# Convolution and phase mixing on one core: two more tiles for the sums, another start-up order

## Chip, cores and metric

The kernel runs on one core of a Trainium2 chip, alone on the chip. The metric is the device time of one launch in microseconds (us). The median of five runs before the change is 1427.22 us (1426.32 to 1431.56).

## What is computed

```python
# x: (8, 4224, 192); weight: (8, 7)
w = softmax(weight)                        # 7 taps for each of 8 groups of 24 channels
x = causal_convolution(x, w)               # along the 4224 tokens
theta = x @ w_theta                        # 192 x 192
zr, zi = x * cos(theta), x * sin(theta)
y = w_tok_r @ zr + w_tok_i @ zi            # 4224 x 4224, along the tokens, for each batch and channel
u = x + y
out = u + max(u @ w_ch, 0)                 # 192 x 192
```

Nearly all arithmetic is in `y`: two 4224 x 4224 matrices times 4224 x 1536 (8 batches of 192 channels).

## The kernel before

**Tiling.** The 4224 tokens are cut into 33 *chunks* of 128 tokens for the inner sum, and into 33 output tiles of 128 tokens, handled two at a time as 17 *units*. The 1536 columns are two halves of 768, and each half is worked on in two pieces of 384. A *visit* multiplies one unit with the chunks that are at hand then, at most 11 (`SLOTS`), since that many fit into on-chip memory. Visits 0 to 16 have few chunks each (`FIRST` lets in two chunks at once and then one per visit); later ones have up to 11. A unit is visited several times, and its running sum of four tiles `d` (128 x 768, fp32) goes out to `part` in DRAM between visits (`store`, L754) and comes back for the next one (`load`, L677). A scheme of the Strassen kind saves one eighth of the products: it needs sums of weights (`w`, L570) and of chunks (`t`, L437).

**Stages of a chunk.** POOL (GpSimd) issues loads of a *window* of x (three pieces of 32 tokens, each with 6 tokens of *halo* ahead of it). PE (TensorE) convolves a window by multiplying with `bands`, a banded matrix made of the taps (L321). ACT (ScalarE) and DVE (VectorE) copy the result out of the banks to `xz` (L182 to L184). It is turned by PE (L486; later chunks by DMA), multiplied with `w_theta` (L501), put through sine and cosine on ACT (L406) and multiplied with x on DVE (L416). Then come the sums `t` (L437).

**Weights.** POOL issues loads of the token weights to `st` (L534), and DVE turns them in blocks of 32 x 32 to `w` (L556).

**Products and outputs.** L715 issues the products, each 128 x 128 by 384 columns. DVE adds a finished bank to `d` (L739). After a unit's last visit the tile is output: ACT casts it to bf16 (L861) into a *container*, which holds the cast and its transpose; the transpose comes from a DMA that ACT issues (L480), or, in the last four visits, from PE; PE multiplies with `w_ch` (L501), DVE takes the maximum and adds (L880), and SP issues the store (L887). There are 5 containers (`outring`), used in turn, and 8 tiles `d`; late in the kernel two more `d` (`late`) come out of memory that the windows have left. Where a unit gets its x added, POOL loads it (`xr<-xs`, L684) and adds it to `d` (L687).

**What sets the order.** All these steps are objects with an assumed duration and a due time. A planner in the program (`Schedule`) runs through them before anything is emitted, with assumed times at which each engine starts (`START`) and at which transfers land (`LAND`), and emits the instructions of each engine in the order that this plan gives. On the chip each engine's queue is then in that fixed order, and an instruction that has to wait holds up all behind it. While the plan's clock is under 60 us (`WARM`) and PE is free in the plan, it emits small matmuls of a zero tile `noise` (128 columns, L1150) that compute nothing and keep PE active. Ahead of the first convolution stand 18 larger ones (512 columns, L981). The noise of L1150 writes into bank 0, which the products use too.

**Start-up.** DVE clears `masks` (L903) and `noise` (L905). POOL issues the first window of x (L275) and turns `masks` into a banded pattern (L912); DVE makes the taps' softmax out of `weight`, sums `masks` over three blocks (`taps`, L931), finds which of three blocks a row belongs to (`block`, a maximum over all of `masks`, L937), multiplies (`terms`, L954), adds over the 7 taps (L963), and scales by `block` to `bands` (L974 on DVE, L972 on ACT).

Of the kernel before, what the change touches and what calls it, by code (L numbers as in the profile page):

```python
# [16 lines left out]
def kernel(  # L17
# [22 lines left out]
    nc = tc.nc  # L40
# [57 lines left out]
    dpool = ctx.enter_context(tc.tile_pool(name="dpool", bufs=8))  # L98
# [113 lines left out]
    bands = constp.tile([WR, H, NQ + WQ, Q], BF16, name="bands")  # L212
# [31 lines left out]

    class Window:
# [15 lines left out]
        def halos(self):  # L261
            prev = self.prev
            for j in range(WQ):
                t0, lo = tokens(*divmod(self.m * WQ + j, NQ)) - KS + 1, j * ROWS
                if t0 < 0:
                    nc.vector.memset(xw[self.k][0 : KS - 1, :, :], 0.0)
                elif self.m < 2:
                    self.loads.append(self.load(lo, t0, KS - 1, prev))
                else:
                    self.loads.append(self.halo(j, lo, prev))  # L270
            self.uses += self.loads

        def load(self, lo, t0, n, prev):
# [6 lines left out]
            if self.m < 2:  # L280
                run()
                s = Step("none", 0.0, None)
                s.fixed = START["x"][self.m]
                return s
# [13 lines left out]
        def conv(self):  # L298
# [29 lines left out]
            for hp in range(H // 2):  # L328
                m = Step(
                    "pe", 0.17, lambda b, hp=hp: conv(b, hp), [self.loads, prevs], mm=True  # L330
# [305 lines left out]
    dtile = tiles(dpool, 8, [P, HN], F32, "d")  # L636
    dfree = [(lambda k=k: dtile[k], []) for k in range(8)]

    def container(k):
        if ("u", k) not in late:  # L640
            if k < 4:
                small_tile(0)
                tag, bufs = (("ang", 2), ("xz", 3))[k % 2]
# [8 lines left out]
    outring = Ring(5)  # L652
    last_of_part = {}

    class Visit:
# [104 lines left out]
        def products(self):  # L760
# [4 lines left out]
            for r in "xys" if self.pair else "xy":  # L765
                for g in gs:
                    k, uses[r, g], prev[r, g] = rings[r].take()
                    rows[r, g] = 2 * "xys".index(r) + k
                    if self.v == 0 and r == "x":
                        continue  # L770
# [83 lines left out]
        def output(self, q):  # L854
            k, use, prev = outring.take()
            if len(outring.uses) <= 5:
                prev = [
                    s for r in ("xz", "uT", "xw") for u in rings[r].uses[-3:] for s in u
                ]
# [36 lines left out]
    START = {"x": (7.5, 10.5), "pe": 7.5, "dve": 10.5, "act": 8.3, "pool": 8.3, "sp": 4.5, "wth": 9.0}  # L896
# [5 lines left out]
    masks = wk.tile([WR, KS, WQ, Q], BF16, name="masks", tag="ang")  # L902
    nc.vector.memset(masks, 1.0)  # L903
    noise = wk.tile([P, 512], BF16, name="noise", tag="ang")
    nc.vector.memset(noise, 0.0)  # L905
    wth_f = wk.tile([P, 4, D], F32, name="wth_f", tag="xz", bufs=3)
    nc.vector.memset(wth_f[:, 1:3, :], 0.0)
# [8 lines left out]
    windows[0].halos()  # L916
    Window()
    ident = constp.tile([P, P], BF16, name="ident")
    make_identity(nc, ident)
    windows[1].halos()  # L920
    nc.vector.memset(bands[:, :, WQ, :], 0.0)
    wmax, wsum, wrcp = (taps_f[:, 1, k * H : (k + 1) * H] for k in range(3))
    nc.vector.tensor_reduce(out=wmax, in_=wsb, axis=mybir.AxisListType.X, op=ALU.max)
    nc.vector.tensor_tensor(
        out=wsb, in0=wsb, in1=wmax[:, :].unsqueeze(2).to_broadcast([P, H, KS]),
        op=ALU.subtract,
    )
    nc.scalar.activation(out=wsb, in_=wsb, func=AT.Exp)
    taps = wk.tile([WR, KS, Q], BF16, name="taps", tag="xz", bufs=3)
    for j in range(1, WQ):  # L930
        nc.vector.tensor_tensor(  # L931
            out=taps, in0=masks[:, :, 0, :] if j == 1 else taps, in1=masks[:, :, j, :],
            op=ALU.add,
        )

    block = constp.tile([WR, WQ], F32, name="block")
    nc.vector.tensor_reduce(  # L937
        out=block, in_=masks[:, :, :, :].rearrange("p k j m -> p j k m"),
        axis=mybir.AxisListType.XY, op=ALU.max,
    )  # L940
    nc.scalar.activation(out=wmax[:, 0:1], in_=wsb[:, 0, 0:1], func=AT.Sin)
    wth_t = wk.tile([P, 4, D], BF16, name="wth", tag="wc", bufs=1)
    nc.scalar.activation(out=wth_t, in_=wth_f, func=AT.Copy)
    nc.vector.tensor_reduce(out=wsum, in_=wsb, axis=mybir.AxisListType.X, op=ALU.add)
    nc.vector.tensor_scalar_add(out=wsum, in0=wsum, scalar1=1e-9)
    nc.vector.reciprocal(out=wrcp, in_=wsum)
    wbf = wk.tile([P, H, KS], BF16, name="wbf", tag="xr")
    nc.vector.tensor_tensor(
        out=wbf, in0=wsb, in1=wrcp[:, :].unsqueeze(2).to_broadcast([P, H, KS]),
        op=ALU.mult,  # L950
    )
    terms = spool.tile([WR, KS, H, Q], BF16, name="terms", tag="st")
    for hs in (slice(0, H // 2), slice(H // 2, H)):
        nc.vector.tensor_tensor(  # L954
            out=terms[:, :, hs], in0=taps[:, :, :].unsqueeze(2).to_broadcast([WR, KS, H // 2, Q]),
            in1=wbf[0:WR, hs, :].rearrange("p h k -> p k h").unsqueeze(3).to_broadcast(
                [WR, KS, H // 2, Q]
            ), op=ALU.mult,
        )
        n = KS  # L960
        while n > 1:
            k = n // 2
            nc.vector.tensor_tensor(  # L963
                out=terms[:, 0:k, hs], in0=terms[:, 0:k, hs], in1=terms[:, n - k : n, hs],
                op=ALU.add,
            )
            n -= k
        for j in (1, 0, 2):
            o = bands[:, hs, j::NQ, :]
            i = terms[:, 0, hs].unsqueeze(2).to_broadcast([WR, H // 2, 2, Q])  # L970
            if j == 1:
                nc.scalar.activation(out=o, in_=i, func=AT.Copy, scale=block[:, j : j + 1])  # L972
            else:
                nc.vector.tensor_scalar_mul(out=o, in0=i, scalar1=block[:, j : j + 1])  # L974
    wth = lambda: wth_t
    wth_ready = Step("none", 0.0, None)
    wth_ready.fixed = START["wth"]

    for k in range(6):
        for _ in range(3):  # L980
            pe(nc.tensor.matmul(banks[k], lhsT=noise[:, 0:P], rhs=noise, start=True, stop=True))  # L981
# [62 lines left out]
    class Schedule:  # L1044


        def __init__(self, emit):
# [13 lines left out]
            self.lent = {k: 0.0 for k in range(2, 6)}  # L1061
# [54 lines left out]
        def step(self, now):  # L1116
# [30 lines left out]
            if now < WARM and self.free["pe"] <= now + 1e-9:  # L1147
                self.free["pe"] = now + 0.11
                if self.emit:
                    pe(nc.tensor.matmul(  # L1150
                        banks[0][:, 3 * P : 4 * P], lhsT=noise[:, 0:P], rhs=noise[:, 0:P],
                        start=False, stop=True, skip_group_check=True,
# [39 lines left out]
```

## Time and profile before

| | |
|---|---|
| median of 5 runs | 1427.22 us |
| the profiled execution: its time / its span | 1425.21 / 1423.5 us |
| PE busy (matmul), weight loads | 1402.1 us (98%), 892.4 us |
| DVE, ACT, POOL busy | 1039.6, 438.3, 508.0 us |
| products (L715) | 3186 + 2228 + 2162 matmuls, 326 ns each, one begun every 163 ns |
| first convolution, first product begun at | 10.76, 19.26 us |
| last noise matmuls begun at | 61.5 us |
| mean granted PE clock | 0.997 |

A line of the windows view gives a stretch of the span, its length, then for each engine the busy time and, in brackets, the number of instructions, the clock granted to PE (1.00 is full speed), the share of time in which the 16 DMA engines were busy, and GB/s. A line of the timeline gives start, duration, engine, source line, operation, tiles and count, and in square brackets how long the engine had been idle and what released it. A line of the waits gives who waited for whom, the total, the number of times and the longest, in us. The release is inferred: where a wait has several causes, only the one that came last by the profile is named.

### The profile page before, as it was taken

To read this page: it belongs to the slowest core of one execution; us is meant where nothing else is said; L and a number is where in the kernel's file an instruction comes from. 1 tells how busy PE (TensorE), PEld (TensorE's weight loads), DVE (VectorE), ACT (ScalarE), POOL (GpSimd) and SP (SyncE) were. 2 spreads that over 40 slices of the span, in tenths; PEclk is the share of its full clock that TensorE was granted. 3 is DMA by queue.
4 is the path that set the end of the run, shared out by engine and by line. 5 is a ranking of instruction groups with operands and counts; after the bars stand their busy time and mean duration, and the time that the engine had idled before them with its cause. 6 is when DMAs were issued, how large, how long until landed. Compare 5 with 4: busy or idle time off the path is not lost.

```text
span 1423.5 us, 25083 instructions
## 1 busy us (share of the span) xinstructions
PE 1402.1 (98%) x9485; PEld 892.4 (63%) x9485; DVE 1039.6 (73%) x1679; ACT 438.3 (31%) x885; POOL 508.0 (36%) x761
## 2 busy tenths in 40 slices
PE   8999999999999999999999999999999999999998
PEld 5666666666666666666666666666666665666665
DVE  7978665345777886776667688687687987887787
ACT  7875522113523323310000342233231212211232
POOL 7543311122432553223213346424545153531120
PEclk9999999999999999999999999999999999999999
DMA  9999975577999899999778999999998999999994
GB/s 132 228 203 203 168 148 105 115 129 166 221 224 237 215 229 243 225 198 216 183 166 206 226 232 241 220 256 218 219 239 168 239 227 217 268 253 197 217 247 145
DMA packets 335777, 291.43 MB, mean 205 GB/s; under 512 B 157140, under 2 KB 284500, under 8 KB 335656
## 3 DMA queue, kind: packets, MB, share of 16 engines
q0 software_dynamic: 168784, 97.61, 50.7%
q1 hardware_dynamic: 126872, 182.39, 40.9%
q10 hardware_dynamic: 40000, 9.84, 5.3%
q8 instruction: 74, 1.21, 0.3%
q14 instruction: 47, 0.39, 0.1%
HBM read 248.53 MB, written 104.99 MB: 248 GB/s over the span
## 4 chain that ended last, share of the span: by engine, by line
PE 94%; DVE 3%; DMA 2%; ACT 1%; issue 1%; POOL 1%; DVEq 0%; POOLq 0%; ACTq 0%
PE bank L715 85%; PE bank L501 6%; PE bank L321 2%; DMA ubT<-ubT 1%; PE bank L486 1%; PE bank L1150 1%; DMA out_dram<-d 0%; DVE d L880 0%; DVE d L739 0%; POOL xw L275 0%; DVE w L570 0%; DVE w L556 0%; DVE i L416 0%; ACT uT L184 0%; DVE xz L182 0%
## 5 line engine op out<-in xcount | busy, mean ns | idle before, releaser
L715 PEld LDWEIGHTS <-w 128*128 128x128 bf16 x7576 | 735.8, 98 | 458.7 <-issue 6.2
L715 PE MATMUL bank<-t,w 128*128 128x384 bf16 x3186 | 563.5, 326 | 3.3 <-DVE d L739 2.9
L739 DVE TENSOR_TENSOR d<-bank,d 128x384 f32<-128x384 f32 x528 | 285.7, 548 | 240.8 <-PE bank L715 206.6
L715 PE MATMUL bank<-i,w 128*128 128x384 bf16 x2228 | 390.6, 326 | 0.2 <-DVE bank L182 0.2
L556 DVE STREAM_TRANSPOSE w<-st 128x640 bf16<-128x640 bf16 (+4 forms) x412 | 341.3, 854 | 66.2 <-PE bank L715 53.4
L715 PE MATMUL bank<-r,w 128*128 128x384 bf16 x2162 | 388.1, 326 | 0.3
L534 POOL DMA_DIRECT2D st<-in_moe_w_tok_r_dram x240 | 137.9, 582 | 438.4 <-DVE w L556 414.3
L570 DVE TENSOR_TENSOR w<-w 128x1408 bf16<-128x1408 bf16 (+8 forms) x212 | 183.9, 867 | 2.6
L534 POOL DMA_DIRECT2D st<-in_moe_w_tok_i_dram x240 | 137.3, 579 | 130.9 <-DVE w L556 118.9
L184 ACT ACTIVATE xz<-bank 64x384 bf16<-64x384 f32 (+2 forms) x297 | 138.3, 482 | 90.6 <-issue 52.4
L275 POOL DMA_DIRECT2D xw<-in_x_dram x137 | 79.5, 587 | 177.7 <-PE bank L321 147.1
L687 POOL TENSOR_TENSOR d<-d,xr 128x768 f32<-128x768 f32 x61 | 103.6, 1700 | 100.6 <-DMA xr<-xs 54.4
L406 ACT ACTIVATE r<-bank,half_pi 128x384 bf16<-128x384 f32 x88 | 47.8, 581 | 263.4 <-PE bank L501 263.2
L184 ACT ACTIVATE bank<-bank 128x384 f32<-128x384 f32 x108 | 51.3, 477 | 219.2 <-PE bank L715 204.2
L184 ACT ACTIVATE d<-bank 128x384 f32<-128x384 f32 x122 | 59.3, 491 | 139.3 <-PE bank L715 138.5
L861 ACT ACTIVATE ubT<-d 128x768 bf16<-128x768 f32 x43 | 36.3, 844 | 146.8 <-DVE d L739 132.0
L880 DVE SCALAR_TENSOR_TENSOR d<-bank,d 128x384 f32<-128x384 f32 x106 | 54.5, 549 | 14.2 <-PE bank L501 12.4
L501 PEld LDWEIGHTS <-uT 128*128 128x128 bf16 x632 | 54.4, 98 | 12.8 <-issue 1.2
L406 ACT ACTIVATE i<-bank 128x384 bf16<-128x384 f32 x132 | 61.7, 495 | 0.0
L501 PE MATMUL bank<-wth,uT 128*128 128x192 bf16 x528 | 56.9, 246 | 0.3
L321 PE MATMUL bank<-xw,bands 114*128 114x192 bf16 x352 | 52.2, 248 | 4.3 <-DMA xw<-in_x_dram 3.2
L501 PE MATMUL bank<-wch,ubT 128*128 128x192 bf16 x424 | 45.9, 246 | 2.4 <-DMA ubT<-ubT 1.3
(75 smaller groups left out, 537.2 us busy)
## 6 DMA issues: line engine op xcount, KB each, us to landing
part<-d SPq DMA_DIRECT2D x168, 384.0 KB
d<-part SPq DMA_DIRECT2D x155, 384.0 KB
st<-in_moe_w_tok_r_dram POOLq DMA_DIRECT2D x156, 176.0 KB, 6.7
st<-in_moe_w_tok_i_dram POOLq DMA_DIRECT2D x156, 176.0 KB, 7.8
out_dram<-d SPq DMA_DIRECT2D x53, 384.0 KB
xw<-in_x_dram POOLq DMA_DIRECT2D x132, 96.0 KB, 4.7
xs<-xz SPq DMA_DIRECT2D x132, 96.0 KB
xr<-xs POOLq DMA_DIRECT2D x66, 192.0 KB, 6.4
```

What stands on the lines that cost most here:

```text
L184: act(nc.scalar.activation(out=o(), in_=i(*b), func=AT.Copy))
L275: pool(nc.gpsimd.dma_start(out=xw[self.k][lo : lo + n, :, :], in_=x[:, t0 : t0 + n, :].rearrange("b s d -> s b d"),))
L321: pe(nc.tensor.matmul(banks[b][:, hh * B * G : (hh + 1) * B * G], lhsT=bands[:, h, at : at + NQ, :].rearrange("p z m -> p (z m)"), rhs=xw[ ...
L406: act(nc.scalar.activation(out=z[:, cols], in_=banks[b][:, 0 : 2 * D], func=AT.Sin, **({"bias": half_pi[:], "scale": 1.0} if i == 0 else { ...
L501: pe(nc.tensor.matmul(banks[bk][:, b * D : (b + 1) * D], lhsT=tT[:, 3 * k + b + i, :], rhs=w[:, 2 * b + i, :], start=(i == 0), stop=(i == ...
L534: "pool", 0.58, lambda a=a, t0=t0, i=i, w=w: pool(nc.gpsimd.dma_start(out=st[i][a * Q : (a + 1) * Q, 0:nb, 0 : n * Q], in_=w[r0 : r0 + nb ...
L556: lambda c=c, ce=ce: dve(nc.vector.transpose(self.tile(name)[:, c:ce, :, :], st[i][:, at : at + NQ, c * Q : ce * Q].rearrange("p bt (c j) ...
L570: s = Step("dve", 0.15 + 0.069 * n, lambda: dve(nc.vector.tensor_tensor(out=flat(self.tile(name)), in0=flat(self.tile(p)), in1=flat(self.t ...
L687: a = Step("pool", 1.75, lambda: pool(nc.gpsimd.tensor_tensor(out=tile_(), in0=tile_(), in1=xrt[k], op=ALU.add)), [r, s])
L715: pe(nc.tensor.matmul(banks[bank][:, 0:PC], lhsT=self.w.block(a, c), rhs=chunks[c].operand(b, g), start=(start and c == self.lo), stop=(c ...
L739: dve(nc.vector.tensor_tensor(out=o, in0=y, in1=o, op=ALU.add))
L880: dve(nc.vector.scalar_tensor_tensor(out=dk, in0=banks[b][:, 0:PC], scalar=0.0, in1=dk, op0=ALU.max, op1=ALU.add,))
```

## The change

1. The tiles `d` become 10 instead of 8. The memory comes from the tag `ang` (two tiles, which held `masks`, `noise` and two of the containers). `masks` and `noise` move to tiles of other tags, and there are 4 containers instead of 5: one in the place of `bands`, two `xz`, one `uT`.
2. `block` is made on POOL, by a memset and two selects of 114 x 3, and no longer by DVE's maximum over `masks`.
3. Two of the three halos of window 1 are copied on the chip by SP out of window 0, instead of loaded by POOL from DRAM. `ident`, the identity for transposes, is made after the loads of window 1.
4. The start-up's DVE and ACT instructions are put into the fixed order (`dve(...)`, `act(...)`), and the loops that build `bands` go over the two halves of the heads in turn.
5. The first noise is 16 matmuls over all banks. Noise of the plan goes into one of the two banks that the plan uses for convolution and mixing, and only when the plan has that bank free. For window 0 and 1 and chunk 0 the plan may lend six banks instead of four.
6. `START` has other times, and the convolutions wait in the plan for `bands`.

```diff
-    dpool = ctx.enter_context(tc.tile_pool(name="dpool", bufs=8))
+    dpool = ctx.enter_context(tc.tile_pool(name="dpool", bufs=10))
...
-    bands = constp.tile([WR, H, NQ + WQ, Q], BF16, name="bands")
+    bands = wk.tile([WR, H, NQ + WQ, Q], BF16, name="bands", tag="bands", bufs=1)
...
-                elif self.m < 2:
+                elif self.m * WQ + j < NQ:
                     self.loads.append(self.load(lo, t0, KS - 1, prev))
...
-                    "pe", 0.17, lambda b, hp=hp: conv(b, hp), [self.loads, prevs], mm=True
+                    "pe", 0.17, lambda b, hp=hp: conv(b, hp), [self.loads, prevs, bands_ready],
+                    mm=True
...
-    dtile = tiles(dpool, 8, [P, HN], F32, "d")
-    dfree = [(lambda k=k: dtile[k], []) for k in range(8)]
+    dtile = tiles(dpool, 10, [P, HN], F32, "d")
+    dfree = [(lambda k=k: dtile[k], []) for k in range(10)]
...
-            if k < 4:
+            if k < 3:
                 small_tile(0)
-                tag, bufs = (("ang", 2), ("xz", 3))[k % 2]
+                tag, bufs = (('bands', 1), ('xz', 3), ('xz', 3))[k]
...
-    outring = Ring(5)
+    outring = Ring(4)
...
-                    if self.v == 0 and r == "x":
-                        continue
...
-            if len(outring.uses) <= 5:
+            if len(outring.uses) <= 4:
...
-    START = {"x": (7.5, 10.5), "pe": 7.5, "dve": 10.5, "act": 8.3, "pool": 8.3, "sp": 4.5, "wth": 9.0}
+    START = {
+        "x0": 6.3, "x1": 10.0, "bands": 9.8, "pe": 8.3, "dve": 9.6, "act": 9.8,
+        "pool": 8.4, "sp": 4.5,
+        "wth": 9.0,
+    }
...
-    masks = wk.tile([WR, KS, WQ, Q], BF16, name="masks", tag="ang")
-    nc.vector.memset(masks, 1.0)
-    noise = wk.tile([P, 512], BF16, name="noise", tag="ang")
-    nc.vector.memset(noise, 0.0)
+    noise = wk.tile([P, 512], BF16, name="noise", tag="xr")
+    dve(nc.vector.memset(noise, 0.0))
+    masks = wk.tile([WR, KS, WQ, Q], BF16, name="masks", tag="xz", bufs=3)
+    dve(nc.vector.memset(masks, 1.0))
...
     windows[0].halos()
+    block = constp.tile([WR, WQ], F32, name="block")
+    nc.gpsimd.memset(block, 1.0)
+    for sign, base in ((1, 0), (-1, ROWS - 1)):
+        nc.gpsimd.affine_select(
+            out=block, in_=block, pattern=[[-sign * ROWS, WQ]],
+            channel_multiplier=sign, base=base, compare_op=ALU.is_ge, fill=0.0,
+        )
     Window()
+    windows[1].halos()
     ident = constp.tile([P, P], BF16, name="ident")
     make_identity(nc, ident)
-    windows[1].halos()
...
-    block = constp.tile([WR, WQ], F32, name="block")
-    nc.vector.tensor_reduce(
-        out=block, in_=masks[:, :, :, :].rearrange("p k j m -> p j k m"),
-        axis=mybir.AxisListType.XY, op=ALU.max,
-    )
...
+    for k in (*range(8), *range(8)):
+        pe(nc.tensor.matmul(banks[k], lhsT=noise[:, 0:P], rhs=noise, start=True, stop=True))
...
-    for k in range(6):
-        for _ in range(3):
-            pe(nc.tensor.matmul(banks[k], lhsT=noise[:, 0:P], rhs=noise, start=True, stop=True))
...
-            self.lent = {k: 0.0 for k in range(2, 6)}
+            self.lent = {k: 0.0 for k in range(6)}
...
-            if now < WARM and self.free["pe"] <= now + 1e-9:
+            b = min(self.mm, key=lambda b: self.mm[b])
+            if now < WARM and self.free["pe"] <= now + 1e-9 and self.mm[b] <= now + 1e-9:
                 self.free["pe"] = now + 0.11
                 if self.emit:
                     pe(nc.tensor.matmul(
-                        banks[0][:, 3 * P : 4 * P], lhsT=noise[:, 0:P], rhs=noise[:, 0:P],
-                        start=False, stop=True, skip_group_check=True,
+                        banks[b][:, 0:P], lhsT=noise[:, 0:P], rhs=noise[:, 0:P],
+                        start=True, stop=True,
                     ))
```

## The prediction

> **What bounds the kernel now.** I read the stretches of the span first, then the waits of PE, then the timeline of the start-up and of the one large stall. In the stretches:
>
> ```profile
> 0.00:10.70 10.70, 5.63 (x20) 2.23 (x20) 8.40 (x25) 4.40 (x7) 9.52 (x20) 1.00 0.73 95
> 10.70:30.00 19.30, 18.33 (x202) 15.25 (x203) 11.97 (x26) 16.05 (x35) 15.50 (x28) 0.91 1.21 144
> 30.00:60.00 30.00, 27.53 (x248) 19.63 (x247) 27.11 (x56) 25.67 (x56) 14.30 (x25) 1.00 1.08 207
> 60.00:180.00 120.00, 119.00 (x867) 78.30 (x865) 91.11 (x158) 80.31 (x172) 48.59 (x85) 1.00 1.01 197
> 180.00:1100.00 920.00, 919.72 (x5957) 573.13 (x5956) 640.33 (x957) 241.97 (x521) 330.11 (x474) 1.00 0.93 202
> 1100.00:1160.00 60.00, 59.52 (x410) 38.48 (x409) 53.04 (x88) 12.72 (x18) 20.93 (x29) 1.00 1.19 241
> 1160.00:1220.00 60.00, 55.74 (x373) 35.44 (x371) 44.58 (x75) 10.08 (x14) 24.19 (x34) 0.97 1.16 225
> 1220.00:1400.00 180.00, 180.00 (x1273) 118.26 (x1272) 145.69 (x264) 43.09 (x61) 44.83 (x69) 1.00 1.08 223
> 1400.00:1423.50 23.50, 16.66 (x151) 11.71 (x148) 17.39 (x34) 3.97 (x5) 0.00 (x0) 0.96 0.58 180
> ```
>
> From 60 to 1400 PE's first number all but equals the length. The change removes none of its real work, so time can only come from three places: the head (0 to 60), the gap of 4.3 us in 1160 to 1220, and the tail (6.8 us idle after 1400). In the head PE looks busy, but with noise: 18 wide noise matmuls fill 1.97 to 7.5, and in the chain of work from 10.7 to 62 noise (L1150) holds 14.2% of 51.3 us, 7.3 us. There ACT and DVE set the pace: 25.7 and 27.1 busy in 30 us. The waits of PE name what is left:
>
> ```profile
> PE bank L321 <- DMA xw<-in_x_dram: 3.2, 1, 3.2
> PE bank L715 <- DVE d L739: 2.9, 1, 2.9
> ...
> PE bank L501 <- DMA ubT<-ubT: 1.3, 1, 1.3
> ```
>
> **Head: bands.** The timeline of the start-up:
>
> ```profile
> 5.71 0.85 DVE L937 TENSOR_REDUCE block<-masks 114x3 f32<-114x672 bf16 x1
> 6.47 0.27 DVE L931 TENSOR_TENSOR taps<-taps,masks 114x224 bf16<-114x224 bf16 x1
> 6.78 2.19 DVE L954 TENSOR_TENSOR terms<-taps,wbf 114x896 bf16<-114x896 bf16 x2
> ...
> 8.89 1.38 DVE L963 TENSOR_TENSOR terms<-terms 114x384 bf16<-114x384 bf16 x6
> ...
> 10.76 0.24 PE L321 MATMUL bank<-xw,bands 114*128 114x192 bf16 x1 [3.16 <-DMA xw<-in_x_dram]
> ```
>
> The first convolution is put down to x, but window 0's last halo is issued at 4.84 and lands 3.4 later, at 8.3. `bands` is what is late: ACT makes its first half from 10.16. Also, both multiplications come first and the six additions run as one group: DVE already alternates between the halves. That edit is worth 0, as is putting these instructions into the fixed order. The mask select, too, stays where it was, behind three loads of x; only `ident` and the last halos change places. What does count is `block`: its 0.85 leaves DVE. `bands` is ready 0.85 earlier and the first convolution starts at about 9.9.
>
> On POOL come a memset (0.1, by `half_pi`'s row) and two selects of 114 x 3. No row is that small: the bounds are 0.3 (the memset of `ident`, 0.27) and 1.24 (the select of `ident`); I take 0.6. The Trainium skill, page "SBUF — State Buffer", section "SBUF: two separate sides", says that DVE work with two SBUF inputs and a GpSimd instruction that reads SBUF shut each other out for a whole instruction. `ident`'s select (128 elements, 1.24 us, beside `terms`) against the mask's (672 elements, 0.94) fits that; by the rule each select may wait for one multiplication of 1.1. Then the second ends at 6.1 + 0.6 + 2 x 1.24 = 9.2, still ahead of the first scaling (9.3), so nothing is lost on `bands`.
>
> POOL's queue behind it matters more. Mask select until 4.29, two halos to 5.39, memset to 5.5, three loads (0.6 each) and two selects, then window 1's halo: issued at 8.5 (7.9 to 9.8), landing 2.8 later as the row of the old one shows, 11.3. The two halos that move to SP go ahead of its four older copies (0.7 each); their source lands by 6, so they are there in time. Window 1's convolution starts at 11.3 and not at 13.5: today it is held by 21 noise matmuls at half clock (11.53 to 13.74), of which 1 is left. Next on POOL: 9.1 + `ident` 1.5 + four weight loads 2.3 puts window 2's x at 12.9 (before 12.52), landing by 18.7; its convolution starts at 19.6 today and its copies at 20.8 to 21.4, so the chain can move by some 2.2 but hardly more. **I take 0.85 + 1.35 = 2.2** up to here (1.0 to 2.9).
>
> **Head: noise.** After the first convolutions 42 noise matmuls remain of 169 (one within the convolutions not counted), since a noise matmul needs a free mixing bank in the plan. At full clock one holds PE's queue for 0.056 (6 in 0.33): 127 x 0.056 = 7.1, of which 20 are the ones counted above, so 107 x 0.056 = 6.0. Nor does noise write bank 0 any more, where it waited for DVE's copies (1.3 + 0.6 in the waits of PE). Against this: ACT has only 5.5 us idle in 15 to 60, so most of the time that noise gives back turns into PE waiting for ACT or DVE. I take 1.8, a third of either (0 to 5.5). Head: **4.0** (1.0 to 8.4).
>
> The page "TensorE: Matmul & The Clock Gate", section "HAM oscillation — how this bites in real kernels", speaks against removing noise: idle gaps of PE over about 3.4 us bring the clock down. The trace is stricter:
>
> ```profile
> 1180.00:1182.00 2.00, 0.00 (x0) 1.00 1.27 198
> 1182.00:1183.00 1.00, 0.93 (x5) 0.77 1.29 216
> 1183.00:1184.00 1.00, 1.00 (x5) 0.50 1.16 262
> ```
>
> A gap of 2.92 (1179.1 to 1182.07) is followed by 3.4 us at half clock, and so is the gap of 3.1 ahead of the first convolution (clock 0.50 from 12.5 to 14.8). Gaps of 1.3 do nothing. The new gap ahead of the first convolution: noise starts at 1.35 (its memset is now first), 8 wide at 0.43, 8 at 0.215, 16 narrow at 0.056 end at 7.4; 2.5 us remain to 9.9. By the rule the clock holds, by the trace it lies between 1.3 and 2.9. A drop costs under 1 us, since ACT and DVE pace this part. In 20 to 30, where noise goes most, single gaps stay under 2 us. I count 0.
>
> **The stall at 1180.** SP's waits in 1100 to 1424 show how short the tiles `d` are:
>
> ```profile
> SPq L677 <- DMA out_dram<-d: 50.8, 19, 11.3
> SPq L677 <- DMA out_dram<-late: 16.8, 4, 8.6
> ```
>
> Loads of `d` stand 67.6 us at the head of SP's queue until an output has left its tile. Two more tiles (12 with the late ones, instead of 10) take most of that away, and POOL's waits for `d` (13.5 us in 1100 to 1240) with it. But SP is not PE. DVE at the stall:
>
> ```profile
> 1175.61 0.56 DVE L739 TENSOR_TENSOR d<-bank,d 128x384 f32<-128x384 f32 x1 [0.96 <-PE bank L715]
> 1180.59 0.98 DVE L556 STREAM_TRANSPOSE w<-st 128x768 bf16<-128x768 bf16 x1 [4.43 <-DMA st<-in_moe_w_tok_r_dram]
> 1181.49 0.52 DVE L739 TENSOR_TENSOR d<-bank,d 128x384 f32<-128x384 f32 x1
> ```
>
> The addition that PE waits for starts 0.90 after the transpose ahead of it, as such pairs do elsewhere (1161.97, 1162.87): it was late because weights were late, not only because `d` was. Freed of `d`, the same stall could stand. The weights were late by queueing on POOL (2.7 us behind `xr`) and by full DMA queues; more tiles let loads of `d` spread out, which relieves both partly. At stake: 2.9 + 1.3 idle, and half clock for 3.4 us (1.6). Of these 5.8 I take 2.5 (0 to 5.8).
>
> **Containers.** Four, used in turn, for 66 outputs in some 300 us: one each 4.5 us, so each may be held for 18. It is held for the cast (0.85), the DMA transpose (up to 13.0, the largest in the chain) and the mix: 15 to 16. Today ACT waits once, for 1.4, on the mix of an older output. Cost taken: 0.3 (0 to 10, see the rivals).
>
> **Tail.** By the order of PE's queue, 56 mixing and 30 transposing matmuls stand behind the last product instead of 60 and 36: one transposition and half a mix less of the alternation with DVE (each about 0.5 + 0.57), while that work moves among products (10 x 0.08). Gain 1.0 (−1 to 2).
>
> **Other edits.** `wbf` on 114 rows, the tags of `masks` and `noise`, the banks lent at the start: nothing, as long as the convolution waits for `bands` and x. `START` changes only the order. The rest of the order, 60 to 1100, moves too; PE there has 0.3 to 1 us idle in all and no wait within sight, so 0 (loss up to 2).
>
> **Sum.** 4.0 + 2.5 − 0.3 + 1.0 = 7.2. Span 1423.5 − 7.2 = 1416.3; with the 1.7 us around the span 1418.0. The profiled execution was 2.0 under the median of the runs, so the forecast is 1427.2 − 7.2 = 1420.0.
>
> **Rivals.**
> A. The gains are hidden: noise only filled what ACT and DVE leave, POOL's two selects cost what the halos save, and the late weights keep the stall. Only `bands` (0.85) and a little of the tail stay: 1426. For it: ACT's 86% and DVE's 90% in 30 to 60, and the DVE row at 1180.59. Against it: 21 noise matmuls alone hold 2.2 us of the chain. Chance 0.15.
> B. All of it comes: head 8.4 and stall 5.8: 14.2, so 1413. For it: SP's 67.6 us, 7.3 us of noise in the chain. Chance 0.2.
> C. Slower: the ring of four containers. ACT's queue is in order, so a cast that waits for its container holds back the copies from bank to bank (L184) that PE's next products read. It decides where a container is held for over four times the spacing of the outputs: from 1117 to 1163 these come every 3.8 us, so at 15.2, which the transpose of 13.0 reaches. Four stalls like those seen (1.3, or 2.9 with 1.6 of half clock: 2.9 in the mean) make 11.6 against the sum of 7.2: 1431.6. For it: transposes of 13 us. Against it: only 1 wait in 50 with five. Chance 0.13.
> The forecast has 0.52.
>
> Within 0.2% (2.9 us), about what a measurement of this kernel can tell from no change, means 1424.3 to 1430.1. Forecast: 0.46 faster, 0.06 same. A: 0.06 and 0.09. B: 0.2 faster. C: 0.02 same, 0.11 slower. Together 0.72, 0.17, 0.11. The range, 1412 to 1428, leaves out most of C and the far end of B.
>
> **What would show it.** Right: first convolution near 9.9, window 1's near 11.3, first product two to three us earlier, noise (L1150) x59, the wait for `out_dram<-d` at SP well under 50 us, no PE wait of 2.9 near 1180. Wrong: the clock at 0.5 within 15 to 40, ACT's L861 waiting for PE's L501 more than a few times, new PE waits for `bank` copies after 1100, or a DVE wait for `st` at another place with PE idle behind it.

## The result and the profile after

The median of 28 runs of the changed kernel is 1420.69 us (1416.9 to 1431.8), beside 1427.02 us of the kernel before in the same series: a ratio of 0.9959, 95% interval 0.9945 to 0.9973, so 3.9 to 7.8 us faster. The profiled execution took 1419.5 us with a span of 1417.8, 5.7 us less than the span of before; the mean granted clock is 0.997 as before. The stretches of the changed kernel:

```profile
0.00:10.70 10.70, 7.46 (x40) 3.55 (x40) 8.57 (x27) 5.28 (x9) 9.49 (x23) 1.00 0.74 97
10.70:30.00 19.30, 15.12 (x139) 12.10 (x140) 13.81 (x29) 15.26 (x33) 14.74 (x26) 0.91 1.26 160
30.00:60.00 30.00, 26.91 (x207) 17.14 (x205) 27.32 (x57) 27.42 (x60) 15.90 (x28) 1.00 1.15 226
...
1100.00:1160.00 60.00, 59.68 (x416) 38.89 (x414) 52.84 (x93) 11.74 (x17) 22.01 (x31) 1.00 1.09 230
1160.00:1220.00 60.00, 59.98 (x417) 39.17 (x416) 46.01 (x83) 10.89 (x15) 27.68 (x37) 1.00 1.20 247
1220.00:1400.00 180.00, 177.32 (x1249) 116.06 (x1247) 145.59 (x262) 42.71 (x61) 39.72 (x62) 0.99 1.08 217
1400.00:1417.80 17.80, 11.03 (x104) 7.79 (x101) 12.57 (x24) 3.46 (x5) 0.00 (x0) 0.92 0.56 177
```

Three things are to be seen. In 10.7 to 60, PE is *less* busy than before (42.0 against 45.9 us) and yet further on: it was noise that went. In 1160 to 1220 the gap of 4.3 us is closed. But in 1220 to 1400, where PE had no idle time, 2.7 us are missing now.

Since noise counts as busy, I measure progress by the **work done** by a time: the products begun by then times 0.1625 us, convolutions and mixing times 0.0825, transposes times 0.056 (each the spacing of such matmuls at full clock), without noise. Both kernels have the same work to do.

| work done in, us | 0–180 | 180–1100 | 1100–1160 | 1160–1220 | 1220–1280 | 1280–1400 | idle after 1400 |
|---|---|---|---|---|---|---|---|
| before | 148.8 | 919.0 | 58.7 | 53.7 | 59.9 | 120.0 | 6.84 |
| after | 152.2 | 919.1 | 59.2 | 59.8 | 55.4 | 120.0 | 6.77 |
| difference | 3.4 | 0.1 | 0.5 | 6.1 | −4.5 | 0.0 | 0.1 |

That makes 3.4 from the head, 2.1 from 1100 to 1400 and 0.1 from the tail, 5.6 of the 5.7 us.

**The head.** In the timeline of the start-up of the changed kernel, the two selects of `block` on POOL, then the scaling and PE's convolutions:

```profile
6.05 0.87 POOL L926 TENSOR_SCALAR_AFFINE_SELECT block<-block 114x3 f32<-114x3 f32 x1
...
7.48 0.45 POOL L926 TENSOR_SCALAR_AFFINE_SELECT block<-block 114x3 f32<-114x3 f32 x1
7.80 1.30 DVE L973 TENSOR_TENSOR terms<-terms 114x384 bf16<-114x384 bf16 x6
7.88 1.16 POOL L280 DMA_DIRECT2D xw<-in_x_dram  x2
...
9.06 0.91 ACT L983 ACTIVATE bands<-terms,block 114x256 bf16<-114x256 bf16 x2 [0.88 <-DVE terms L973]
...
9.66 0.96 PE L324 MATMUL bank<-xw,bands 114*128 114x192 bf16 x8 [1.89 <-ACT bands L983]
...
11.29 0.49 PE L324 MATMUL bank<-xw,bands 114*128 114x192 bf16 x4 [0.67 <-DMA xw<-in_x_dram]
```

`block` is ready at 7.93, before `terms` is. The selects, however, stand ahead of window 1's last loads on POOL (7.88 to 9.04), so that window 1 is convolved 0.67 us after PE has run out of window 0. Each select lasts until a multiplication of DVE that runs beside it is over:

```profile
5.79 1.09 DVE L963 TENSOR_TENSOR terms<-taps,wbf 114x896 bf16<-114x896 bf16 x1
...
6.80 1.08 DVE L963 TENSOR_TENSOR terms<-taps,wbf 114x896 bf16<-114x896 bf16 x1
```

These end at 6.88 and 7.88, the selects at 6.92 and 7.93.

The first transposes begin at 13.15 (15.81 before), the first product only at 19.03 (19.26 before). The mixing and the first product, of the kernel before, then of the changed one:

```profile
16.98 1.56 PE L501 MATMUL bank<-wth,uT 128*128 128x192 bf16 x16
...
19.26 0.48 PE L715 MATMUL bank<-r,w 128*128 128x384 bf16 x2
```

```profile
15.07 1.72 PE L505 MATMUL bank<-wth,uT 128*128 128x192 bf16 x16
...
19.03 1.03 PE L719 MATMUL bank<-r,w 128*128 128x384 bf16 x4 [0.56 <-DVE t L441]
```

The mixing comes 1.9 us earlier, the product 0.2. Before, the product begins when DVE's first `r` is done (18.65 to 19.21); in the new order it begins when `t` is done (18.46 to 19.02), the sum that DVE makes after both `r`. The clock fell to 0.5 here, from 12 to 15.5, as it did before the change.

**The stall.** PE's waits that answer to those of before:

```profile
PE bank L719 <- DVE d L743: 2.7, 1, 2.7
...
PE bank L324 <- ACT bands L983: 1.9, 1, 1.9
...
PE bank L324 <- DMA xw<-in_x_dram: 0.7, 1, 0.7
```

There is still one wait for an addition, now at 1224. The timelines of DVE and PE there:

```profile
1220.90 0.56 DVE L743 TENSOR_TENSOR d<-bank,d 128x384 f32<-128x384 f32 x1 [0.88 <-PE bank L719]
1224.93 1.70 DVE L560 STREAM_TRANSPOSE w<-st 128x768 bf16<-128x768 bf16 x2 [3.46 <-DMA st<-in_moe_w_tok_r_dram]
1226.56 0.52 DVE L743 TENSOR_TENSOR d<-bank,d 128x384 f32<-128x384 f32 x1
```

```profile
1222.49 1.95 PE L719 MATMUL bank<-t,w 128*128 128x384 bf16 x11
1227.13 3.55 PE L719 MATMUL bank<-t,w 128*128 128x384 bf16 x11 [2.68 <-DVE d L743]
```

It is the stall of before in another place: DVE's queue reaches a transpose whose weights have not landed, and the addition behind it, whose bank is long full, waits too. The chain of waits names the load, started at 1209.50 after POOL had waited for a free `st`:

```profile
1207.76 1.38 POOL st L538 x3
1209.14 0.36 issue
1209.50 15.30 DMA st<-in_moe_w_tok_r_dram
```

15.3 us, where the plan reckons with 8 (`LAND["w"]`). The granted clock is 0.64, 0.50 and 0.57 in 1227 to 1228, to 1229 and to 1231. SP's waits for outputs, in 1100 to 1418:

```profile
SPq L681 <- DMA out_dram<-d: 54.7, 25, 6.2
SPq L681 <- DMA out_dram<-late: 12.4, 6, 3.8
```

The sum is 67.1 us, against 67.6: no less. Only the longest wait is shorter (6.2 against 11.3).

### The profile page after: what moved, and what is told of

It reads as the page before. It is cut to its first block, busy times and chain, and to the rows that moved or that the text cites. A ratio compares the mean times of both kernels' runs of the same rounds, so it can differ in the third digit from the quotient of the medians.

```text
span 1417.8 us, 24835 instructions
## 1 busy us (share of the span) xinstructions
PE 1396.3 (98%) x9371; PEld 885.8 (62%) x9371; DVE 1028.4 (73%) x1676; ACT 438.1 (31%) x887; POOL 505.9 (36%) x762
## 4 chain that ended last, share of the span: by engine, by line
PE 93%; DMA 3%; DVE 1%; ACT 1%; POOL 1%; issue 0%; DVEq 0%; POOLq 0%; ACTq 0%
PE bank L719 85%; PE bank L505 5%; PE bank L324 2%; DMA st<-in_moe_w_tok_r_dram 2%; PE bank L490 1%; DMA st<-in_moe_w_tok_i_dram 0%; DMA ubT<-ubT 0%; POOL xw L280 0%; DVE w L560 0%; ACT xz L184 0%; ACT r L410 0%; POOL st L538 0%; DVE d L882 0%; ACT uT L184 0%; DMA xw<-in_x_dram 0%
## 5 line engine op out<-in xcount | busy, mean ns | idle before, releaser
L574 DVE TENSOR_TENSOR w<-w 128x1408 bf16<-128x1408 bf16 (+8 forms) x212 | 178.3, 841 | 2.6
L280 POOL DMA_DIRECT2D xw<-in_x_dram x135 | 78.4, 587 | 207.7 <-PE bank L324 166.2
L691 POOL TENSOR_TENSOR d<-d,xr 128x768 f32<-128x768 f32 x60 | 100.6, 1678 | 61.7 <-DMA xr<-xs 33.2
L184 ACT ACTIVATE d<-bank 128x384 f32<-128x384 f32 x123 | 59.9, 491 | 138.1 <-PE bank L719 136.1
L324 PEld LDWEIGHTS <-bands 114*128 114x128 bf16 x352 | 33.0, 98 | 23.4 <-issue 4.8
```

The source lines that it names most:

```text
L184: act(nc.scalar.activation(out=o(), in_=i(*b), func=AT.Copy))
L280: pool(nc.gpsimd.dma_start(out=xw[self.k][lo : lo + n, :, :], in_=x[:, t0 : t0 + n, :].rearrange("b s d -> s b d"),))
L324: pe(nc.tensor.matmul(banks[b][:, hh * B * G : (hh + 1) * B * G], lhsT=bands[:, h, at : at + NQ, :].rearrange("p z m -> p (z m)"), rhs=xw[ ...
L574: s = Step("dve", 0.15 + 0.069 * n, lambda: dve(nc.vector.tensor_tensor(out=flat(self.tile(name)), in0=flat(self.tile(p)), in1=flat(self.t ...
L691: a = Step("pool", 1.75, lambda: pool(nc.gpsimd.tensor_tensor(out=tile_(), in0=tile_(), in1=xrt[k], op=ALU.add)), [r, s])
```

## The experiments

The theory: the head gains because noise left PE's in-order queue and the start-up became shorter; the two tiles `d` only shift a stall that late weights make. Rivals: the start-up edits alone make the gain; noise only fills idle time, so that removing it is free and gives nothing; the tiles make the gain. Work is that of the profiled execution of each. The kernel before had medians of 1425.96 (first group, four kernels), 1427.14 (second) and 1426.95 us (third) in these series.

| kernel | median us | ratio to before, 95% | work 0–180 | work 1100–1400 | clock 12–15 |
|---|---|---|---|---|---|
| before | | | 148.8 | 292.3 | 0.50 |
| after | 1420.69 | 0.9959 [0.9945, 0.9973] | 152.2 | 294.4 | 0.52 |
| 1 head_only | 1424.78 | 0.9990 [0.9966, 1.0013] | 153.2 | 294.2 | 1.00 |
| 1 tiles_only | 1424.95 | 0.9990 [0.9975, 1.0006] | 149.0 | 294.0 | 1.00 |
| 1 noise_back | 1426.18 | 0.9990 [0.9972, 1.0009] | 149.6 | 292.2 | 1.00 |
| 1 block_back | 1421.85 | 0.9959 [0.9942, 0.9976] | 152.9 | 286.8 | 1.00 |
| 2 no_noise | 1424.87 | 0.9995 [0.9970, 1.0021] | 150.2 | 292.5 | 0.50 |
| 2 before_no_noise | 1430.54 | 1.0007 [0.9978, 1.0036] | 149.0 | 290.4 | 0.52 |
| 2 st3_d8 | 1426.10 | 1.0005 [0.9986, 1.0023] | 154.7 | 288.4 | 1.00 |
| 2 land14 | 1450.29 | 1.0158 [1.0112, 1.0204] | 139.8 | 280.9 | 0.64 |
| 3 block_late | 1421.18 | 0.9979 [0.9953, 1.0005] | 153.5 | 291.3 | 1.00 |
| 3 land14_late | 1430.56 | 1.0023 [0.9999, 1.0048] | 151.9 | 283.4 | 0.57 |
| 3 both | 1425.48 | 1.0002 [0.9969, 1.0034] | 153.4 | 276.7 | 1.00 |
| 3 d9_ring5 | 1423.09 | 0.9970 [0.9943, 0.9996] | 153.2 | 296.1 | 1.00 |

The work up to 180 is steady: the five kernels with the new noise that kept the full clock, two `st` and an unchanged plan for the first weights lie at 152.9 to 153.5. That of 1100 to 1400 is one draw out of a wide spread. The changed kernel, block_back and block_late have the same order on PE, DVE and ACT from the first convolution to the end, and yet 294.4, 286.8 and 291.3 us of work there; land14_late and `both` share an order too, with 283.4 and 276.7. So a difference of some 7 us in this column proves nothing. In d9_ring5 the profiled execution (1415.4 us) was the fastest of 12 that reach to 1431.0. So I read the head by the work, and the later part by rows and by the ratios.

The head's share is seen in the ratios too, where the memory is the same. Of the kernels with ten `d`, four containers and two `st` that keep the plan's landing times, the three with the head's gain (the changed kernel, block_back, block_late) are at 0.9959, 0.9959 and 0.9979. The three that lack most of it (tiles_only, noise_back, no_noise) are at 0.9990, 0.9990 and 0.9995. That is some 3.7 us in the mean, and 3.3 us in the work by 180 us.

### Head alone, tiles alone

head_only is the changed kernel with 8 tiles `d` and 5 containers:

```diff
-    dtile = tiles(dpool, 10, [P, HN], F32, "d")
+    dtile = tiles(dpool, 8, [P, HN], F32, "d")
...
-                tag, bufs = (('bands', 1), ('xz', 3), ('xz', 3))[k]
+                tag, bufs = (('bands', 1), ('xz', 3), ('ang', 1), ('xz', 3))[k]
...
-    outring = Ring(4)
+    outring = Ring(5)
```

> The new start-up with the old memory (8 tiles d, 5 containers). If the head's gain is a matter of the start-up alone, the work that PE has done by 180 us stands about 3.4 us ahead of before, as it does with the whole change, and the end comes 3 to 4 us under before (1423.5). If the output phase is short of tiles d, SP's waits for out_dram stay at 60 to 70 us and a PE stall of 3 to 6 us stays after 1100. If the stall there comes from late weights whatever the tiles, it is there too, but at any place.

tiles_only is the kernel before with 10 `d`, 4 containers and the tags of part 1 of the change:

```diff
-    dtile = tiles(dpool, 8, [P, HN], F32, "d")
+    dtile = tiles(dpool, 10, [P, HN], F32, "d")
...
-    outring = Ring(5)
+    outring = Ring(4)
```

> The old start-up with the new memory (10 tiles d, 4 containers). If the tiles d are what PE waits for after 1100: no stall over 1 us there, 4 to 6 us gained, 1422. If weights that land late are the cause: a stall of the same kind (PE behind a DVE addition that stands behind a transpose of w waiting for st), 0 to 2 us gained, 1426. If the ring of four containers costs by itself: ACT waits for mixes (L501), 1429 or more.

Measured: by work, the head's gain is all in head_only (153.2) and none of it in tiles_only (149.0). By the medians each part alone gives 1.0 to 1.2 us, and both intervals hold 1. So the 3 to 4 us that were expected of head_only did not come in its time (its interval reaches from 4.8 us faster to 1.9 slower), and where its 4.4 us of work go later is not shown. The interval of tiles_only lies just above that of the whole change: the new memory alone does not make the gain. The product of the two ratios is 0.998; the lower ends multiply to 0.994, so the 0.9959 of both together does not contradict a plain sum. A gain from the two acting together is neither shown nor excluded. In tiles_only the stall is there too (PE's wait for a `d` addition, 3.4 us, after 1220), as in head_only (1.6 us, and 2.4 for an output's transpose, both in 1160 to 1220).

### Noise back, and noise gone

noise_back is the changed kernel with the noise of before, its condition and its bank:

```diff
-            if now < WARM and self.free["pe"] <= now + 1e-9 and self.mm[b] <= now + 1e-9:
+            if now < WARM and self.free["pe"] <= now + 1e-9:
...
-                        banks[b][:, 0:P], lhsT=noise[:, 0:P], rhs=noise[:, 0:P],
-                        start=True, stop=True,
+                        banks[0][:, 3 * P : 4 * P], lhsT=noise[:, 0:P], rhs=noise[:, 0:P],
+                        start=False, stop=True, skip_group_check=True,
```

> The change with the noise of before: unconditional in the plan and written into bank 0. If noise in PE's queue held the chain, the first 180 us lose 1.5 to 2.5 us against the change, 1422.5. If noise only filled time in which PE would have waited for ACT and DVE, nothing is lost in the head (under 0.5), 1420.7; if the clock was the use of noise, the granted clock from 15 to 40 is higher than with the change and the head gains.

Nearly all of the head's gain is gone: 149.6 against 153.2 in head_only, both at full clock throughout the start. So the condition and the choice of bank are worth 3.6 us together. They were not tried apart, and noise_back has a clash of its own: the new plan lends bank 0 to window 0 and 1 and to chunk 0, and the noise goes into bank 0 as well. Three times in the first 19 us PE stands with noise at the head of its queue until that bank is read out:

```profile
12.93 0.61 PE L1160 MATMUL bank<-noise 128*128 128x128 bf16 x8 [0.65 <-DVE xz L182]
...
16.92 0.89 PE L1160 MATMUL bank<-noise 128*128 128x128 bf16 x13 [0.67 <-ACT r L410]
...
18.83 0.77 PE L1160 MATMUL bank<-noise 128*128 128x128 bf16 x11 [0.58 <-ACT i L410]
```

Neither the kernel before nor tiles_only has these 1.9 us. If all of them are lost time, 1.7 of the 3.6 are left for the noise as it was before; that is an estimate. The stretch 30 to 60, first of noise_back, then of head_only:

```profile
30.00:60.00 30.00, 27.53 (x250) 19.65 (x248) 27.17 (x55) 25.50 (x56) 15.26 (x27) 1.00 1.11 218
```

```profile
30.00:60.00 30.00, 26.89 (x208) 17.20 (x207) 27.33 (x56) 27.62 (x60) 17.00 (x30) 1.00 1.15 223
```

Without the noise PE is less busy and ACT gets 2.1 us more done: noise matmuls had stood in PE's queue ahead of the mixing and transposes that ACT waits for, and had waited for bank 0 themselves (0.62, 0.66 and 0.66 us, at 31.66, 37.66 and 52.72, as in the kernel before).

The other side: no_noise ends the plan's noise before the first convolution (16 of 59 remain), and before_no_noise does the same to the kernel before (2 of 171 remain):

```diff
-    EARLY, SLACK, CALM, WARM = {}, 12.0, 30.0, 60.0
+    EARLY, SLACK, CALM, WARM = {}, 12.0, 30.0, 11.0
```

(8.0 in before_no_noise.)

> The change without the 43 small noise matmuls that are left after the first convolution. If noise costs where it stands in the chain: another 0.5 to 1 us by 180 us (153 to 154). If the rest is harmless filler: no change (152.2 to 153.2). If the clock needs it: half clock between 12 and 25 and 1 to 2 us lost.

> The kernel before with one edit: after the first convolution the plan emits no more noise (20 matmuls of zeros remain of 189). If noise in PE's queue held the head's chain, PE's work by 180 us stands at 152 to 153 (before 148.8), nearly all of the head's gain, and the end comes 3 to 4 us earlier, 1422.5. If noise only filled idle time, it stays at 149 to 149.5. If the clock needs it, the granted clock falls to half somewhere in 15 to 60 and the work by 180 us falls under 148.

no_noise does 2.0 us less work than the changed kernel and 3.0 less than head_only. Its clock tells why; from 12 to 30:

```profile
12.00:15.00 3.00, 2.56 (x20) 1.84 (x18) 2.95 (x7) 2.26 (x5) 3.00 (x6) 0.50 1.14 163
15.00:20.00 5.00, 3.93 (x22) 2.64 (x21) 2.72 (x6) 4.51 (x10) 4.29 (x9) 0.66 1.40 156
20.00:25.00 5.00, 3.54 (x27) 2.88 (x26) 3.91 (x9) 3.15 (x7) 5.00 (x10) 0.68 1.28 172
25.00:30.00 5.00, 4.23 (x32) 2.76 (x30) 3.15 (x7) 4.66 (x12) 1.10 (x2) 0.98 1.13 165
```

In the changed kernel the clock is 0.94 in 15 to 20 and 1.00 from there on. before_no_noise is at 0.61, 0.73 and 0.58 in 15 to 20, 20 to 25 and 25 to 30: the clock is low for longer, and the removal brings nothing in sum (149.0 against 148.8). So noise is neither free nor useless. 43 noise matmuls in gaps of the plan and in banks that are free keep the clock and are worth 2 to 3 us; the other hundred or so, in bank 0 and in front of work, cost up to 3.6.

### `block` back on DVE, and behind window 1

block_back drops POOL's memset and selects and restores DVE's maximum:

```diff
-    nc.gpsimd.memset(block, 1.0)
...
+    dve(nc.vector.tensor_reduce(
+        out=block, in_=masks[:, :, :, :].rearrange("p k j m -> p j k m"),
+        axis=mybir.AxisListType.XY, op=ALU.max,
+    ))
```

> The change with block made by DVE's maximum over masks again and no selects on POOL. If bands decide the head: first convolution 0.85 later (10.5) and all of it lost in the first 180 us, 1421.5. If window 1's x decides (it landed at 11.25 with the change, held by POOL's two selects of 0.87 and 0.45): window 1's convolution starts at 11.0 to 11.3 as before the undoing, and less than 0.4 is lost.

PE's timeline there:

```profile
10.46 1.26 PE L324 MATMUL bank<-xw,bands 114*128 114x192 bf16 x12 [2.61 <-DMA xw<-in_x_dram]
11.56 0.22 PE L1159 MATMUL bank<-noise 128*128 128x128 bf16 x1
11.62 0.49 PE L324 MATMUL bank<-xw,bands 114*128 114x192 bf16 x4
```

The first convolution is 0.8 later than in the changed kernel, but 12 run through, since window 1's x is no longer behind the selects. The transposes begin at 13.06. That is no later than in the changed kernel (13.15), but there the clock was at half; in head_only, at full clock as here, they begin at 12.66. The work by 180 is 152.9 against 153.2, and the ratio is that of the changed kernel, 0.9959. So the move of `block` by itself is worth some tenths at most, less than these runs can tell: most of what it gives to `bands` it takes from x.

block_late has the memset and selects on POOL behind window 1's loads:

```diff
     Window()
     windows[1].halos()
+    block = constp.tile([WR, WQ], F32, name="block")
+    nc.gpsimd.memset(block, 1.0)
...
```

> The changed kernel with the memset and the two selects for block put behind window 1's loads and halo on GpSimd, in place of ahead of them. Theory: window 1's x is issued some 1.4 us earlier and lands near 9.9, and bands is as early as before the edit unless block's selects now come after the first scaling needs them (they end near 8.6, bands is scaled from 8.8), so all 24 convolutions of the first two windows run through from 9.7 and the work done by 180 us is 0.5 to 1.2 us more: 1419.5 to 1420.2. Rival: what paces the head from there is ACT and DVE (banks copied to xz), so nothing but a smaller gap comes of it: work at 180 within 0.3 of the changed kernel's, 1420.7.

All of window 1's loads are issued by 7.75, the selects take 0.41 and 0.22 and end at 9.1, the convolutions start at 10.01 and 12 run through. The work at 180 is 153.5. That is 1.3 more than in the changed kernel, as the theory had it, but the changed kernel's profile had the low clock. Against head_only and d9_ring5, at full clock, it is 0.3 more, and the median (1421.18) is no lower than that of the changed kernel: no gain beyond the clock is shown.

### Weights that land late

land14 raises the plan's landing time of weights from 8 to 14 us everywhere, land14_late only for the weights made in the plan after 1050 us, and `both` adds that to block_late; st3_d8 has three tiles `st` and pays with `d` (8).

> The change with one number of the plan altered: weights are assumed to land 14 us after their issue, not 8. If the stall after 1100 comes from transposes that the plan places on DVE before their weights have landed (12 to 18 us there), with the additions behind them: no DVE wait for st over 2 us after 1100, no PE wait for d over 1 us, 4 us gained, 1416.5. If transfers are late because the DMA queues are full, whatever the plan: a stall of the same kind at another place, 1420.7.

> The changed kernel, the plan's landing time of weights 14 us instead of 8 only for weights made in the plan after 1050 us; everything up to there is emitted in the same order. Theory (weights that land late hold a transpose on VectorE, and the additions queued behind it hold PE): VectorE's waits for st after 1100 fall under 1 us, the PE waits for an addition go with them, and work from 1100 to 1400 is 2 to 4 us more: 1417 to 1419. Rival (something is late in any order, since loads, tiles and outputs compete for the same DMA queues): the stall moves to other causes, outputs or d, and the time is 1420 to 1424.

> Both of the edits, block behind window 1's loads and late weights planned at 14 us. Theory: the two are apart in time and add up: 1416 to 1418.5. Rival: neither holds, 1420 to 1424.

> The change with a third tile st for the weights on their way and 8 tiles d (and 4 containers). If the stall after 1100 comes from weights whose load is issued late because a tile st is not free: DVE's waits for st and PE's wait for a d addition vanish there, and the end comes 2 to 5 us under the change, 1417, even with two tiles d less. If the tiles d carry the gain of the output phase: SP's waits for out_dram go up to over 65 us and the end is at 1423 or more.

The edits of land14_late and of st3_d8:

```diff
-                        )), [prev], lands=LAND["w"], wire=nb * Q * (21 + 4.8 * n) / 16e3,
+                        )), [prev], lands=LAND["w"] if at < 1050 else 14.0, wire=nb * Q * (21 + 4.8 * n) / 16e3,
```

```diff
-    stt = tiles(spool, 2, [P, 2 * NQ, SLOTS * Q], BF16, "st")
+    stt = tiles(spool, 3, [P, 2 * NQ, SLOTS * Q], BF16, "st")
...
-    dtile = tiles(dpool, 10, [P, HN], F32, "d")
+    dtile = tiles(dpool, 8, [P, HN], F32, "d")
```

land14 is 1.6% slower than before, with 12 us lost in the head already (139.8), where its order of weights and chunks is another one from the start; after 1100 DVE's waits for `st` are gone all but 0.2 us, but others take their place (PE's waits for `w` 3.5, for transposed outputs 7.2). That alone could be put down to the other order of the whole. land14_late leaves everything up to 1095 us in place, and it loses as well: 1430.56. The kernel `both` has 1425.48, above what its theory and its rival expected (1416 to 1418.5, 1420 to 1424). The theory that the plan only has to reckon with late weights falls. POOL's timeline there, then DVE's and PE's:

```profile
1213.53 0.58 POOL L538 DMA_DIRECT2D st<-in_moe_w_tok_r_dram  x1 [0.91 <-DMA st<-in_moe_w_tok_i_dram]
1223.01 2.28 POOL L538 DMA_DIRECT2D st<-in_moe_w_tok_i_dram  x4 [8.90 <-DVE small L574]
```

```profile
1241.56 1.70 DVE L560 STREAM_TRANSPOSE w<-st 128x768 bf16<-128x768 bf16 x2 [2.69 <-DMA st<-in_moe_w_tok_i_dram]
```

```profile
1245.05 6.28 PE L719 MATMUL bank<-t,w 128*128 128x384 bf16 x22 [5.64 <-DVE w L574]
```

A transpose that is planned later holds its `st` longer; there are two of these, so the next load is issued later (POOL waits 8.9 us), takes 16 us again, and now PE lacks the weights themselves. The latency is moved, not covered. A third `st` at the price of two `d` does not help in time either (1426.10): DVE waits 4.8 and 4.4 us for late weights all the same, and SP's waits for outputs are 86.9 us. By 180 us, though, st3_d8 has done the most work of all, 154.7. A third `st` beside ten `d` was not tried.

### Nine tiles, five containers

```diff
-    dtile = tiles(dpool, 10, [P, HN], F32, "d")
+    dtile = tiles(dpool, 9, [P, HN], F32, "d")
...
-    outring = Ring(4)
+    outring = Ring(5)
```

> The changed kernel with 9 tiles d and 5 containers in place of 10 and 4. If two more d are what the output phase gains from, one of them gives half: work from 1100 to 1400 lies between that of 8 and 10 tiles, SP's waits for outputs between 67 and 80 us, time 1421 to 1424. If the containers had been short, ACT's waits for the ring (11 us in sum with four) go and PE's work from 1100 to 1400 rises by over 1 us: under 1420. If neither binds, only the place of a stall changes: 1419 to 1424 with SP's waits unchanged.

The profiled execution of d9_ring5 shows what the order can do when the weights come in time: after 1100 PE's longest kinds of wait are these.

```profile
PE bank L719 <- DVE d L743: 0.7, 2, 0.5
PE bank L505 <- DMA ubT<-ubT: 0.6, 1, 0.6
PE bank L505 <- DVE d L882: 0.6, 2, 0.4
```

Its span is 1413.7, with no stall at all; DVE waits for `st` 4.3 us there in sum, at most 1.3 at a time. Its median is 2.4 above the changed kernel's, and the intervals overlap. The last expectation, that neither `d` nor containers bind, fits best: SP's waits are 78.4 us with 8 `d`, 60.2 with 9 and 67.1 with 10, in no order; in block_back and block_late, with the order of the changed kernel, they are 75.8 and 59.0.

## Why the prediction was right in its time, and where it was wrong

The forecast was 1420.0 us and 0.72 for faster; measured are 1420.69 us and an interval wholly on that side. The sum was 7.2, the profiles give 5.7 and the medians 6.3. Its terms:

- **Bands and window 1** (2.2 of the head). The times were right: first convolution at 9.66 (9.9 expected), window 1's at 11.29 (11.3). The step that failed is "first product two to three us earlier": it came 0.2 earlier (19.03), and from tiles_only (18.11) to head_only (17.91), both at full clock, it is 0.2 too. What the transposes and the mixing had won went into the wait for `t`, since in the new order the first product stands behind that. How much of the 2.2 is left as work is not settled. tiles_only and noise_back, both at full clock, differ in the start-up (with `START` and the lent banks) and by 0.6 us of work, but noise_back pays for the clash over bank 0 as well: by estimate 0.6 to 2.5.
- **Noise** (1.8). The mechanism was right, noise x59 as foreseen and the waits for bank 0 gone. With its bank the noise is worth up to 3.6, by estimate 1.7 without the clash; so 1.8 is neither confirmed nor refuted. Only both terms together are measured: from tiles_only to head_only 4.2, against the 4.0 of the prediction.
- **Clock** (0). The prediction weighed the rule of about 3.4 us of idle time, from the Trainium skill's page "TensorE: Matmul & The Clock Gate" (section "HAM oscillation — how this bites in real kernels"), against the trace's 1.3 to 2.9, and took no drop. It did drop, after 1.89 us and, with 0.96 of convolutions between, another 0.67. The changed kernel and land14_late, both with the drop, have 152.2 and 151.9; block_back, block_late, `both` and d9_ring5, without it and in the same order on PE, DVE and ACT up to 560 us at least, have 152.9 to 153.5. The price is about 1.2, a little over the "under 1 us" of the prediction. Whether it comes is not fixed by the order: the gap ahead of the first convolution was 1.89 us in the changed kernel and 2.33 in land14_late, and from 1.08 (noise_back) to 2.54 (land14) with the same number of noise matmuls ahead of it. The prediction took 8 of the 16 wide ones at 0.43 us; in land14 it was 6, in noise_back 13. With 4.2 − 1.2 = 3.0 and a drop in the kernel before that cost 0.2 (148.8, tiles_only 149.0), the head comes to 3.2, near the 3.4 seen.
- **Selects on POOL.** 0.87 and 0.45 lie within the bounds, near the 0.6 taken. The prediction let each of them wait for a multiplication, by the Trainium skill's page "SBUF — State Buffer" (section "SBUF: two separate sides"), and the trace agrees: each select ends 0.05 us after the multiplication beside it. So it is in all ten kernels with these selects: the 20 selects end 0.04 to 0.06 us after an instruction of DVE with two inputs, and the shortest, begun just before such an end, took 0.20. Measured by that one the two lost some 0.9 us, an estimate, and window 1's x was late by 0.67.
- **The stall** (2.5 of 5.8). "Freed of `d`, the same stall could stand" is what happened, 45 us later: 6.1 won, 4.5 lost. Net 2.1 from 1100 to 1400 with the containers, against 2.2. That the sizes agree is luck: the same order gives 286.8 in block_back and 291.3 in block_late, less than the 292.3 of before. One execution of d9_ring5 has no stall, and the new memory without the new head gives 1.0 us in the median (3.6 faster to 0.9 slower). What the two tiles are worth stays open.
- **SP's waits.** "Should fall well under 50" is wrong: 67.1. The plan issues the loads of `d` as soon as there are tiles for them, so that SP always stands at the next one. A long wait at the head of a queue whose work is early is no cost, and no measure of scarcity. POOL's 13.5 us of waiting for `d` did go (1.4), but it waits 8.3 for `xr` instead.
- **Containers** (0.3). Rival C did not come: ACT's casts wait 9.8 us for a DMA transpose and 1.3 for a mix in the whole kernel, and PE waits for no copy of ACT's after 1100.
- **Tail** (1.0). Wrong: 6.84 to 6.77 us idle after 1400. In every kernel but land14 it is 6.4 to 7.2, whatever the number of `d`; how many matmuls stand behind the last product by the order did not decide it.

## What to carry over

Noise that keeps a clock up has to be put only where the plan has nothing that could run, and into a bank that nothing else needs: too much of it costs as surely as too little, and PE's busy share hides both. Count the real work done by a time, not the busy time. And a stall whose releaser is a late load is not removed by more room elsewhere: look at the row ahead of the late instruction on its own engine, ask what frees the tile that the load goes to, and don't judge such a part by one profile: two executions of one order lay over 7 us apart in one stage.

## What was not expected of the hardware

- The clock went down after less idle time than the prediction's rows had shown. Ahead of and between the first convolutions, PE's idle time of 2.43 us in one piece (block_late), of 1.76 + 0.66 (st3_d8) and of 2.61 in one piece (block_back) left it at 1.00; 1.89 + 0.67 (changed kernel) brought 0.5, as did 2.68 in one piece at the stall. So between 2.4 and 2.7 us it goes either way, if the sum counts where short work stands between two gaps, which these rows suggest but don't show. What decides is not seen.
- The loads of weights took 6.8 us in the median and up to 15.8 us after 1100, with the DMA share at 1.1 to 1.2. The runs of one program spread by 15 us (1416.9 to 1431.8), and the profiles differ where such a load is late; that this makes all of the spread is not shown.
- The same small selects on POOL took from 0.20 to 0.87 us, as long as DVE's instruction beside them still had to run. It goes the other way round too: at 369.55 a multiplication of DVE (`t<-xz,t`) takes 1.97 us, where such take 0.55 alone, beside POOL's addition of `xr` to `d` (369.42 to 371.08).
